# A fused FNet and state-space kernel: the stores of ScalarE move to GpSimd and SyncE

## The chip, the cores and the metric

The kernel runs on one core of one Trainium2 chip. The core has five engines, each with its own instruction stream that it works through in order: TensorE (PE) multiplies matrices, VectorE (DVE) and ScalarE (ACT) do elementwise work, GpSimd (POOL) and SyncE (SP) here mostly issue DMA transfers. Every engine but VectorE and TensorE issues transfers in this kernel. An issue is an instruction of the issuing engine's stream: it waits for what the transfer needs, and what stands behind it on that engine waits too. The transfer itself runs on the core's 16 DMA engines.

The metric is the device time of one execution in microseconds (us).

## The reference

Two independent parts of the same shape, 2048 positions by 512 channels in 32-bit floats, whose outputs are put side by side.

```python
def _A_ref(x, dft_seq_re, dft_seq_im, dft_hid_re, dft_hid_im):      # FNet
    a = jnp.einsum("bsd,ed->bse", x, dft_hid_re)
    b = jnp.einsum("bsd,ed->bse", x, dft_hid_im)
    return jnp.einsum("ts,bse->bte", dft_seq_re, a) - jnp.einsum("ts,bse->bte", dft_seq_im, b)

def _B_ref(u, log_A_real, A_imag, C_real, C_imag, log_dt, D_skip):  # state space
    dt = jnp.exp(log_dt)
    A = -jnp.exp(log_A_real) + 1j * A_imag
    C = (C_real + 1j * C_imag) * dt[:, None]
    P = jnp.exp((A * dt[:, None])[:, :, None] * pos[None, None, :])
    K = 2.0 * jnp.einsum("dn,dnl->dl", C, P).real
    y = jnp.fft.irfft(jnp.fft.rfft(u_t, 2 * L) * jnp.fft.rfft(K, 2 * L)[None], 2 * L)[:, :, :L]
    return y.transpose(0, 2, 1) + u * D_skip[None, None, :]
```

The first part is a Fourier transform over positions and channels, of which only the real part is kept, written as matrix products. The second builds a convolution kernel K of length 2048 for every channel out of 128 complex exponentials, and convolves each channel of u with it through a Fourier transform of length 4096.

## The kernel before

**FNet part** (class `Fnet`). Every 32-bit matrix is split into a rounded high part and a remainder (`hi` and `lo`; ACT makes `hi` at L192, DVE `lo` at L196), and a product is three matmuls at L309. There are twelve groups: eight of kind "s" (four column blocks t, real and imaginary part c), which multiply the sequence matrix by x over 16 slices, and four of kind "p", which multiply those results by the hidden matrix over 8 slices. A group keeps four accumulators d in PSUM, one per 128 rows. Its slices come through SP (L280, tile `raw`, four buffers, of 256 KB each); the splits have three buffers. When a group ends, `evacuate` copies each accumulator out (ACT, L323) into a tile `y`, of which there are three buffers, and stores it: an "s" group's into an intermediate tensor `p` (L328), read back later as `raw`, a "p" group's into the output (L331). The next group's first matmul into an accumulator waits for its eviction.

**State-space part** (class `Ssm`). Tables of exponentials are built in 16 chunks of 32 channels by doubling, mostly on DVE (L541, L550, L557 to L570, with seeds from ACT at L585 to L617); two chunks at a time go through TensorE into taps (L738), and through the first stage of the transform (L768), whose result ACT copies into `xk_sb` and four transfers store to an intermediate tensor `xk` (L785). In the first 100 us the inputs u pass the same first stage in eight steps (L814): POOL loads them (L808), ACT evicts, two transfers per tile store to `xu` (L831). Then for each quarter h of the channels and each q of four groups of frequencies: POOL loads `xu` and `xk` in transposed order (L878), TensorE does the second stage (L907), ACT evicts (L918), DVE multiplies the spectra (L929 to L945), TensorE runs the first inverse stage (L952), ACT evicts into `z` (L967) and two transfers store to `zs` (L973). The last stage loads `zs` (POOL; L1000 for h below 3, L1008 for h = 3, one fetch per q), multiplies (L1023), evicts and stores to the output (L1041; L1034 for h = 3). Tile `z` has one buffer for h below 3 and two for h = 3, and the same buffers hold a product of the spectra in between.

**The order of the work.** All of this is written as Python generators that yield what they need next: an engine with an estimated duration, a buffer, or an event. The class `Plan` runs them on its own clock and emits the instructions in the order in which the plan starts them. So each engine's stream is fixed beforehand. Transfers are one resource in the plan, "dma", whichever engine issues them: a change of the issuing engine leaves the planned order as it is, and moves the instruction into another engine's stream at the same place of that order.

**Who issues what before.** SP issues the slices (`raw`) and constants, POOL the loads of the state-space part (L532 for parameters, L808, L878, L1000, L1008) and eight small additions (L761), ACT the stores at L328, L331, L785, L831, L973 and L1041, and one transfer at each end (L276, L1034).

Of the kernel before, what the change touches and what calls it, by code (L numbers as in the profile page):

```python
# [153 lines left out]
def act(cols):  # L154
    return 0.09 + cols * 0.00085


def dve(cols, rate=1.0):
    return (62 + cols / rate) / 960


def load(kb):
    return max(0.55, kb / 330)


class Fnet:
# [152 lines left out]
    def evacuate(self, g, d, ps):  # L319
        yield self.ys  # L320
        y = self.pool.tile([128, DM], F32, name="y", bufs=STAGED)
        yield "act", act(512)
        self.nc.scalar.activation(y, ps, AF.Copy, scale=-1.0 if g[2] == 1 else 1.0)  # L323
        self.plan.put(self.acc)
        yield "dma", load(256)
        kind, t, c = g
        if kind == "s":
            self.nc.scalar.dma_start(self.p[t, c, d], y)  # L328
            self.plan.set(self.p_ev[t, c, d])
        else:  # L330
            self.nc.scalar.dma_start(self.out[128 * d:128 * d + 128, 512 * t:512 * t + 512], y)  # L331
        self.plan.put(self.ys)


# [27 lines left out]
class Ssm:  # L362
# [393 lines left out]
    def stage1_k(self, ks, n, ev):  # L756

        nc = self.nc
        yield ev
        yield "pool", 0.2  # L760
        nc.gpsimd.tensor_tensor(ks[:, :, 0], self.dskip[:, 16 * n:16 * n + 16], ks[:, :, 0], op=OP.add)  # L761
        yield self.const_ev
        got = yield from self.banks(2)
        yield "pe", 1.82
        for a in range(2):
            for j in range(4):
                r = slice(32 * j, 32 * j + 32)
                nc.tensor.matmul(got[j // 2][1][:, j % 2], self.f1k[r, a], ks[r, :, 32 * a:32 * a + 32],  # L768
                                 start=a == 0, stop=a == 1, tile_position=(32 * j, 0))
        self.plan.put(self.kss)  # L770
        if n == 7:
            self.plan.set(self.k_ev)
        yield self.xks
        xs = self.tab.tile([128, 32, 64], F32, name="xk_sb")
        for h, (k, p) in enumerate(got):
            for j in range(2):
                yield "act", act(512)
                o = 32 * h + 16 * j
                nc.scalar.activation(xs[:, :, o:o + 16], p[:, j].rearrange("p (i l) -> p l i", i=16), AF.Copy)
            self.give(k)  # L780
        xk = self.xk[n // 2].rearrange("b l c s d -> b (c s) l d")[..., 64 * (n % 2):64 * (n % 2) + 64]
        yield "dma", load(1400)
        for k in range(4):
            l = slice(16 * (k // 2), 16 * (k // 2) + 16)
            nc.scalar.dma_start(xk[k % 2, :, l], xs[64 * (k % 2):64 * (k % 2) + 64, l])  # L785
        self.plan.put(self.xks)
        if n % 2:
            self.plan.set(self.xk_ev[n // 2])
        if n == 7:
            self.plan.set(self.tab_ev)  # L790
# [37 lines left out]
    def store_u(self, x, m, sem):  # L828
        yield "dma", load(512)
        for b in range(2):  # L830
            self.nc.scalar.dma_start(self.xu[b, 2 * m:2 * m + 2].rearrange("l c s d -> (c s) l d"),  # L831
                                     x[64 * b:64 * b + 64])
        self.plan.put(sem)
        self.uleft -= 1
        if not self.uleft:
            self.plan.put(self.zls)
            self.plan.set(self.xu_ev)
# [58 lines left out]
    def product(self, b, h, q, got, done):  # L896
        nc, v, a = self.nc, self.nc.vector, self.nc.scalar
        uk = b.pool.tile([128, 2, 2, 2, 2, PART], F32, name="uk", bufs=b.un)
        yield "pe", 1.86
        for r in range(2):  # L900
            for n, name in enumerate("uk"):
                xt = self.xt[name, h, q]
                for c in range(2):
                    for xx in range(4):
                        for g in range(2):
                            rows, o = slice(64 * g, 64 * g + 64), (2 * n + c) * PART
                            nc.tensor.matmul(got[r][1][32 * xx:32 * xx + 32, g, o:o + PART],  # L907
                                             self.w2[rows, 8 * q + 4 * r + xx, 32 * c:32 * c + 32], xt[rows, r, xx],
                                             start=True, stop=True, tile_position=(64 * g, 32 * xx))
        for name in "uk":  # L910
            self.plan.put(b.xts[name])
        self.plan.set(done)
        u, t = uk[:, :, :, 0], uk[:, :, :, 1]
        evs = [Event(), Event()]

        def evict(r, k, p):
            yield "act", act(1024)
            a.activation(uk[:, r].rearrange("p g n c d -> p g (n c d)"), p, AF.Copy)  # L918
            self.give(k)
            self.plan.set(evs[r])  # L920
        for r in range(2):
            self.plan.spawn(evict(r, *got[r]), 1)
        yield b.zbs
        P = b.pool.tile([128, 2, 2, 2, PART], F32, name="z", bufs=b.zn)
        W = b.pool.tile([128, 2, 2, PART], F32, name="w", bufs=b.n)
        for r in range(2):
            yield evs[r]
            yield "dve", dve(512), *APART
            v.tensor_tensor(P[:, r], t[:, r], u[:, r, 0:1].to_broadcast([128, 2, 2, PART]), op=OP.mult)  # L929
        yield "dve", dve(512), *APART  # L930
        v.tensor_tensor(W, t[:, :, 0], u[:, :, 1], op=OP.mult)
        yield "dve", dve(512)
        v.tensor_tensor(P[:, :, 1], P[:, :, 1], W, op=OP.add)
        yield "dve", dve(512), *APART
        v.tensor_tensor(W, t[:, :, 0], u[:, :, 1, ::-1], op=OP.mult)
        for r in range(2):
            yield "dve", dve(512), *APART
            v.tensor_tensor(t[:, r], t[:, r], u[:, r, 0:1, ::-1].to_broadcast([128, 2, 2, PART]), op=OP.mult)
        yield "dve", dve(512), *APART
        v.tensor_tensor(u[:, :, :, 0], P[:, :, :, 0], P[:, :, :, 1], op=OP.subtract)  # L940
        self.plan.put(b.zbs)
        yield "dve", dve(512), *APART
        v.tensor_tensor(t[:, :, 1], t[:, :, 1], W, op=OP.add)
        yield "dve", dve(512)
        v.tensor_tensor(t[:, :, :, 0], t[:, :, :, 0], t[:, :, :, 1], op=OP.add)  # L945

        def run(got):
            for c, Y in enumerate((u, t)):
                for g in range(2):
                    for xx in range(4):  # L950
                        rows = slice(32 * xx, 32 * xx + 32)
                        nc.tensor.matmul(got[xx // 2][1][64 * g:64 * g + 64, xx % 2, :2 * PART], self.ia[rows, c],  # L952
                                         Y[rows, :, g, 0], start=c == 0, stop=c == 1, tile_position=(32 * xx, 64 * g))
        w = Joined(self, run)
        if self.taps_left > 1:
            self.waiting.append(w)
            yield w
        if w.got is None:
            got = yield from self.banks(2)
            yield "pe", 0.95  # L960
            w.run(got, False)
        self.plan.put(b.uks)
        yield b.zbs
        z = b.pool.tile([128, 2, 4, PART], F32, name="z", bufs=b.zn)
        for n, (k, p) in enumerate(w.got):
            yield "act", act(512)
            a.activation(z[:, :, 2 * n:2 * n + 2].rearrange("p r x d -> p x r d"),  # L967
                         p[:, :, :2 * PART].rearrange("p x (r d) -> p x r d", r=2), AF.Copy)
            w.leave(k)
        view = self.zs[h].rearrange("b s q c l d -> b q (c l) s d")  # L970
        yield "dma", load(512)
        for g in range(2):
            nc.scalar.dma_start(view[g, q], z[64 * g:64 * g + 64].rearrange("p r x d -> p (r x) d"))  # L973
        self.plan.put(b.zbs)
        if h == 3:
            self.plan.set(self.zq_ev[q])
        self.left[h] -= 1
        if not self.left[h]:
            self.plan.set(self.zs_ev[h])
# [34 lines left out]
    def inverse(self, z, h, i):  # L1014

        nc, n, m = self.nc, 16, 4
        (k, ps), = yield from self.banks(1)
        yield "pe", 0.95
        for w in range(m):
            for j in range(4):  # L1020
                for g in range(2):
                    rows, l = slice(64 * g, 64 * g + 64), 4 * w + j
                    nc.tensor.matmul(ps[32 * j:32 * j + 32, g, PART * w:PART * w + PART], self.ib[rows, n * i + l],  # L1023
                                     z[rows, l], start=True, stop=True, tile_position=(64 * g, 32 * j))
        y = self.out[:, :, m * i:m * i + m, PART * h:PART * h + PART]
# [12 lines left out]
            nc.scalar.activation(*part(g), AF.Copy)  # L1038
        self.give(k)
        yield "dma", load(512)  # L1040
        nc.scalar.dma_start(y, z[:, :2 * m].rearrange("p (g w) d -> p g w d", g=2))  # L1041
        self.plan.put(self.zls)


# [76 lines left out]
```

## Time and profile before

| | |
|---|---|
| median of 3 runs | 634.37 us (633.76 to 634.55) |
| profiled execution | 630.61 us, of which the span from the first to the last instruction is 628.8 |
| TensorE busy | 583.5 us, 93% of the span |
| VectorE busy | 537.5 us, 85% |
| ScalarE busy | 378.8 us, 60% |
| GpSimd busy | 50.9 us, 8% |
| moved by DMA | 125.43 MB |
| granted TensorE clock, mean | 0.976 |

In lines of the profile L309 is line 309 of the kernel; `acc<-hi,x_hi` is an instruction that writes tile `acc` and reads `hi` and `x_hi`. PE, PEld, DVE, ACT and POOL are busy times of the engines (PEld is the weight load, which overlaps). A "q" behind an engine's name (ACTq, SPq) marks instructions of its sequencer, such as the issue of a transfer, which aren't counted as busy; the issue on POOL is. "x32" is a count. Behind "|" stand the busy time in us and the mean of one instruction in ns, then the idle time of the engine just before and what ended it. In the view of waits "PE acc L309 <- ACT y L323: 8.6, 7, 4.2" says that PE stood idle before L309 for 8.6 us in 7 cases, the longest of 4.2, until ACT had done L323. In a timeline the columns are start, duration, engine, line, operation, tiles and count, with the idle time before in brackets. In sums by stretches each engine has its busy us and its count of instructions, and behind them stand the granted clock, the DMA share and GB/s.

### The profile page before, as it was taken

How to read it: one execution, taken by the hardware profiler on the slowest of the kernel's cores; microseconds unless marked ns; L12 is line 12 of the kernel's file. 1: busy time of each engine (PE TensorE's matmuls, PEld its weight loads, DVE VectorE, ACT ScalarE, POOL GpSimd, SP SyncE). 2: the span in 40 equal slices, each digit the busy share in tenths (PEclk: the TensorE clock that was granted, in tenths of full speed). 3: DMA queues.
4: the chain of work that ended last, by engine and by line, in shares of the span. 5: the costliest groups of instructions: out<-in, count | busy, mean ns of one | idle time of the engine just before them, and what ended most of it. 6: DMA issues, size and time to landing. Idle time of an engine off the chain costs nothing. (4 is left out here: it accounts for less than half of the span.)

```text
span 628.8 us, 17602 instructions
## 1 busy us (share of the span) xinstructions
PE 583.5 (93%) x7302; PEld 445.7 (71%) x7302; DVE 537.5 (85%) x948; ACT 378.8 (60%) x743; POOL 50.9 (8%) x84
## 2 busy tenths in 40 slices
PE   7999999999899999997999899999999999999862
PEld 4877757777588867885788667867777777776641
DVE  5899959989899999998799899999999999639530
ACT  4589876847756566656474667585765554445330
POOL 0000000000010010010011101000100100030110
PEclk7999999999999999999799999999999999999996
DMA  8899987553473375537576567457788685897685
GB/s 270 280 310 303 314 288 221 171 134 106 106 238 103 93 199 160 176 87 186 174 214 209 144 199 178 131 169 184 227 262 266 186 228 158 227 305 247 176 202 147
DMA packets 107983, 125.43 MB, mean 199 GB/s; under 512 B 40000, under 2 KB 67008, under 8 KB 107648
## 3 DMA queue, kind: packets, MB, share of 16 engines
q1 hardware_dynamic: 31168, 52.74, 27.4%
q10 hardware_dynamic: 68608, 41.43, 24.3%
q0 software_dynamic: 8128, 30.15, 15.6%
q8 instruction: 57, 0.93, 0.6%
q14 instruction: 22, 0.18, 0.1%
HBM read 81.56 MB, written 42.73 MB: 198 GB/s over the span
## 5 line engine op out<-in xcount | busy, mean ns | idle before, releaser
L309 PE MATMUL acc<-hi,x_hi 128*128 128x512 f32 x640 | 261.2, 408 | 14.2 <-ACT y L323 8.6
L309 PE MATMUL acc<-lo,x_hi 128*128 128x512 f32 x640 | 253.1, 395 | 1.8 <-DVE lo L196 1.7
L309 PE MATMUL acc<-hi,x_lo 128*128 128x512 f32 x640 | 252.3, 394 | 0.0
L541 DVE TENSOR_TENSOR prod<-t,cs 128x1024 f32<-128x1024 f32 (+4 forms) x192 | 164.8, 869 | 9.2 <-ACT t L680 5.6
L309 PEld LDWEIGHTS acc<-hi,x_hi 128*128 128x128 f32 x640 | 121.8, 190 | 64.6 <-issue 19.2
L192 ACT ACTIVATE hi<-raw 128x512 fp32r<-128x512 f32 x160 | 99.0, 627 | 96.9 <-PE acc L309 64.2
L196 DVE TENSOR_TENSOR lo<-raw,hi 128x512 fp32r<-128x512 f32 x160 | 108.8, 686 | 40.5 <-ACT hi L192 40.2
L309 PEld LDWEIGHTS acc<-lo,x_hi 128*128 128x128 f32 x640 | 122.0, 191 | 27.7 <-DVE lo L196 4.5
L309 PEld LDWEIGHTS acc<-hi,x_lo 128*128 128x128 f32 x640 | 121.7, 190 | 26.7 <-DVE x_lo L196 0.3
L550 DVE TENSOR_TENSOR t<-prod 128x512 f32<-128x512 f32 (+3 forms) x192 | 94.9, 511 | 1.3
L557 ACT ACTIVATE square<-t 128x256 f32<-128x256 f32 (+1 forms) x64 | 36.6, 571 | 23.1 <-DVE t L550 17.8
L323 ACT ACTIVATE y<-acc 128x512 f32<-128x512 f32 x48 | 28.3, 593 | 16.3 <-PE acc L309 9.3
L918 ACT ACTIVATE uk<-f 128x1024 f32<-128x1024 f32 x32 | 31.6, 1014 | 6.8 <-PE f L907 6.8
L738 PEld LDWEIGHTS f<-t,t 128*32 128x32 f32 x2048 | 29.5, 110 | 8.4 <-issue 5.6
L738 PE MATMUL f<-t,t 128*32 128x64 f32 x2048 | 32.4, 220 | 2.0 <-issue 1.8
L617 ACT ACTIVATE cs<-cs 128x352 f32<-128x352 f32 x32 | 15.4, 535 | 21.6 <-DVE cs L612 21.6
L570 DVE TENSOR_TENSOR t<-square 128x128 f32<-128x128 f32 (+1 forms) x64 | 24.7, 386 | 1.4 <-ACT square L557 1.3
L929 DVE TENSOR_TENSOR z<-uk 128x512 f32<-128x512 f32 x32 | 21.3, 686 | 4.3 <-ACT uk L918 4.0
L967 ACT ACTIVATE z<-f 128x512 f32<-128x512 f32 x32 | 17.5, 588 | 11.7 <-issue 4.6
L878 POOL DMA_DIRECT2D xt_u<-xu x13 | 11.8, 908 | 152.7 <-PE f L907 135.8
L599 ACT ACT_TABLE_LOAD x16 | 20.5, 1283 | 5.4 <-DMA xk<-xk_sb 4.8
L907 PE MATMUL f<-xt_k,w 64*32 64x128 f32 x1088 | 23.1, 271 | 0.5 <-issue 0.5
(100 smaller groups left out, 521.5 us busy)
## 6 DMA issues: line engine op xcount, KB each, us to landing
raw<-in_sT SPq DMA_DIRECT2D x127, 256.0 KB, 3.4
p<-y ACTq DMA_DIRECT2D x32, 256.0 KB, 4.1
xk<-xk_sb ACTq DMA_DIRECT2D x32, 256.0 KB, 5.1
xt_k<-xk POOLq DMA_DIRECT2D x16, 512.0 KB, 6.6
zs<-z ACTq DMA_DIRECT2D x32, 256.0 KB, 4.5
raw<-p SPq DMA_DIRECT2D x32, 256.0 KB, 4.1
xt_u<-xu POOLq DMA_DIRECT2D x13, 512.0 KB, 6.4
zl<-zs POOLq DMA_DIRECT2D x12, 512.0 KB, 6.4
```

Of the source, the lines that this page charges most:

```text
L192: self.nc.scalar.activation(hi, src, AF.Copy)
L196: self.nc.vector.tensor_tensor(lo, src, hi.bitcast(F32), op=OP.subtract)
L309: nc.tensor.matmul(acc[d], l[:, cols], r, start=k == 0 and n == 0, stop=k == len(items) - 1 and n == 2)
L323: self.nc.scalar.activation(y, ps, AF.Copy, scale=-1.0 if g[2] == 1 else 1.0)
L541: self.nc.vector.tensor_tensor(p.rearrange("p k d c m -> p k (d c) m"), src.rearrange("p d c l -> p (d c) l")[:, None, :, rows].to_broadca ...
L550: self.nc.vector.tensor_tensor(dst[:, :, :, rows], p[:, 0], p[:, 1, :, ::-1], op=OP.add)
L557: self.nc.scalar.activation(sq, t[:, :, :, m // 2:m], AF.Square)
L570: self.nc.vector.tensor_tensor(t[:, :, 0, m:2 * m:2], box[0][:, :, 0], box[0][:, :, 1], op=OP.subtract)
L738: nc.tensor.matmul(ps[32 * j:32 * j + 32, i], t1[:, d, c], t2[:, d, c], start=c == 0, stop=c == 1, tile_position=(0, 32 * j))
L907: nc.tensor.matmul(got[r][1][32 * xx:32 * xx + 32, g, o:o + PART], self.w2[rows, 8 * q + 4 * r + xx, 32 * c:32 * c + 32], xt[rows, r, xx], ...
L918: a.activation(uk[:, r].rearrange("p g n c d -> p g (n c d)"), p, AF.Copy)
L929: v.tensor_tensor(P[:, r], t[:, r], u[:, r, 0:1].to_broadcast([128, 2, 2, PART]), op=OP.mult)
```

## The change

Six issues change their engine. The stores of the state-space part (`xk`, `xu`, `zs`, and the output for h below 3) are issued by GpSimd, which issues that part's loads; the stores of `y` are issued by SyncE, which issues the `raw` loads. Sizes, tiles, buffers and the planned order stay. The last store of all (L1034) and the very first load (L276) stay on ScalarE.

```diff
@@ Fnet.evacuate
         if kind == "s":
-            self.nc.scalar.dma_start(self.p[t, c, d], y)
+            self.nc.sync.dma_start(self.p[t, c, d], y)
             self.plan.set(self.p_ev[t, c, d])
         else:
-            self.nc.scalar.dma_start(self.out[128 * d:128 * d + 128, 512 * t:512 * t + 512], y)
+            self.nc.sync.dma_start(self.out[128 * d:128 * d + 128, 512 * t:512 * t + 512], y)
@@ Ssm.stage1_k
-            nc.scalar.dma_start(xk[k % 2, :, l], xs[64 * (k % 2):64 * (k % 2) + 64, l])
+            nc.gpsimd.dma_start(xk[k % 2, :, l], xs[64 * (k % 2):64 * (k % 2) + 64, l])
@@ Ssm.store_u
-            self.nc.scalar.dma_start(self.xu[b, 2 * m:2 * m + 2].rearrange("l c s d -> (c s) l d"),
+            self.nc.gpsimd.dma_start(self.xu[b, 2 * m:2 * m + 2].rearrange("l c s d -> (c s) l d"),
                                      x[64 * b:64 * b + 64])
@@ Ssm.product
-            nc.scalar.dma_start(view[g, q], z[64 * g:64 * g + 64].rearrange("p r x d -> p (r x) d"))
+            nc.gpsimd.dma_start(view[g, q], z[64 * g:64 * g + 64].rearrange("p r x d -> p (r x) d"))
@@ Ssm.inverse
-        nc.scalar.dma_start(y, z[:, :2 * m].rearrange("p (g w) d -> p g w d", g=2))
+        nc.gpsimd.dma_start(y, z[:, :2 * m].rearrange("p (g w) d -> p g w d", g=2))
```

## The prediction

> **What bounds the kernel now.** I read the page first, then the waits of PE and of DVE, then sums by stretches of time, and last the timelines around the longest waits.
>
> ```profile
> span 628.8 us, 17602 instructions
> ...
> 100.00:540.00 440.00, 422.43 (x5591) 328.61 (x5590) 415.19 (x724) 272.64 (x543) 35.50 (x53) 0.99 0.62 176
> ...
> PE f L1023 <- DMA zl<-zs: 13.3, 2, 12.6
> PE acc L309 <- ACT y L323: 8.6, 7, 4.2
> PE f L907 <- ACT z L967: 2.7, 2, 2.2
> PE acc L309 <- ACT hi L192: 2.2, 2, 1.8
> ...
> PE f L814 <- ACT ks L748: 1.1, 1, 1.1
> ...
> DVE prod L541 <- ACT t L680: 5.6, 1, 5.6
> ...
> L196 DVE TENSOR_TENSOR lo<-raw,hi 128x512 fp32r<-128x512 f32 x122 | 82.8, 685 | 17.0 <-ACT hi L192 16.9
> ```
>
> The second line is the stretch from 100 to 540 us: TensorE (PE) is busy 422.4 of 440 us, VectorE (DVE) 415.2, ScalarE (ACT) 272.6. Two engines are nearly full and run in a written order; ACT stands between them and is, by its busy time, far from full. Yet the waits name ACT nearly everywhere: in the middle PE waits for evictions (y L323) and splits (hi L192), and DVE stands 16.9 us behind splits in that stretch. Why an engine with spare time is late shows in its own timeline. A DMA that an engine issues isn't counted as busy, but nothing behind it on that engine starts meanwhile:
>
> ```profile
> 291.22 0.63 ACT L323 ACTIVATE y<-acc 128x512 f32<-128x512 f32 x1
> 291.39 5.24 ACTq L785 DMA_DIRECT2D xk<-xk_sb  x4
> 296.66 1.28 ACT L599 ACT_TABLE_LOAD   x1 [4.82 <-DMA xk<-xk_sb]
> ...
> 298.23 0.58 ACT L323 ACTIVATE y<-acc 128x512 f32<-128x512 f32 x1
> ...
> 298.86 0.80 PE L309 MATMUL acc<-hi,x_hi 128*128 128x512 f32 x1 [4.18 <-ACT y L323]
> 301.08 0.79 PE L309 MATMUL acc<-hi,x_hi 128*128 128x512 f32 x1 [0.57 <-ACT y L323]
> ...
> 236.27 0.50 PE L309 MATMUL acc<-hi,x_hi 128*128 128x512 f32 x1 [1.22 <-ACT y L323]
> 238.31 0.50 PE L309 MATMUL acc<-hi,x_hi 128*128 128x512 f32 x1 [1.08 <-ACT y L323]
> ```
>
> Between two evictions of one group ACT issues the four xk stores for 5.24 us; the next eviction starts at 298.23, and PE, which needs that bank, has stood still for 4.18 us. So the bound is the pair PE and DVE, with ACT's issues as the cause of part of their idle time.
>
> **The change part by part.** What leaves ACT:
>
> ```profile
> L785 ACTq DMA_DIRECT2D xk<-xk_sb x32: 596/928/2274, 124.3 to 549.3; - x32
> L973 ACTq DMA_DIRECT2D zs<-z x32: 582/640/1876, 217.3 to 609.2; - x32
> L831 ACTq DMA_DIRECT2D xu<-zl x22: 582/620/1323, 46.9 to 102.4; - x22
> L328 ACTq DMA_DIRECT2D p<-y x32: 326/331/1513, 55.4 to 476.2; - x32
> ```
>
> By counts and medians (the middle of the three ns): 32 x 0.928 = 29.7, 32 x 0.640 = 20.5, the 32 xu stores (22 from zl, 10 from z, at zl's median) x 0.620 = 19.8, 32 x 0.331 = 10.6; the 16 out_ya and 6 out_yb stores come on top. That is at least 81 us of ACT's order, and most of it costs nothing, because splits run ahead of PE. What counts is where someone waits:
>
> *xk stores (L785).* The four PE gaps above sum to 4.18 + 0.57 + 1.22 + 1.08 = 7.05 us; all stand right behind a block of four issues. One more at 170 us ended by a split is the 1.8 of the row "PE acc L309 <- ACT hi L192". Together 8.8 us. The clock adds to it:
>
> ```profile
> 168.70:172.10 3.40, 1.40 (x6) 0.95 (x6) 1.65 (x3) 2.31 (x6) 0.00 (x0) 1.00 0.88 187
> 172.10:175.50 3.40, 3.40 (x10) 2.65 (x9) 3.40 (x7) 1.82 (x5) 1.32 (x2) 0.50 0.89 237
> ...
> 291.00:298.40 7.40, 3.67 (x17) 2.71 (x15) 5.16 (x9) 2.57 (x5) 0.00 (x0) 1.00 0.86 199
> 298.40:305.20 6.80, 5.77 (x13) 4.08 (x14) 4.54 (x7) 4.30 (x9) 0.56 (x1) 0.50 0.82 262
> ```
>
> The first number behind the stretch's length is PE's busy time; the seventh column is the granted clock. After each of the two stretches in which PE was less than half busy the clock is 0.50, for 3.4 and 6.8 us. Half of the busy time there is lost: (3.40 + 5.77) / 2 = 4.6 us. No gap, no such stretch.
>
> *xu stores (L831).* They hold up PE once for 1.1 us (L814) and DVE once for 5.6 us (L541 behind t L680).
>
> So PE is offered 8.8 + 4.6 + 1.1 = 14.5 us. Will DVE follow? It is idle for 440 - 415.2 = 24.8 us in the long stretch, 16.9 of it behind splits; without those some 8 us of idle time are left, so DVE could follow for about 15 us, but then both engines would be without slack at the same time, and each late handover then costs. Ends: 0 (all comes back as waits of PE for DVE) and 14.5. I take two thirds, 9.7 us, nearer to the upper row because in the three largest gaps PE and DVE stand idle together.
>
> *What the stores cost on GpSimd (POOL).* No store is issued there in this trace. The nearest rows:
>
> ```profile
> L878 POOL DMA_DIRECT2D xt_k<-xk x16: 531/561/578, 174.1 to 556.3; - x16
> L878 POOL DMA_DIRECT2D xt_u<-xu x13: 894/907/937, 108.3 to 533.1; - x13
> ...
> zs<-z ACTq DMA_DIRECT2D x32, 256.0 KB, 4.5
> raw<-p SPq DMA_DIRECT2D x32, 256.0 KB, 4.1
> ...
> zl<-zs POOLq DMA_DIRECT2D x8, 256.0 KB, 5.0
> ...
> sum 629.00, PE 583.49 PEld 445.69 DVE 537.48 ACT 378.79 POOL 50.88; mean PE 145.87 PEld 111.42 DVE 134.37 ACT 94.70 POOL 12.72
> ```
>
> A transfer in long rows takes POOL 0.56 us, one in 1024 rows of 512 bytes 0.91. An xk store has 1024 pieces, zs 512, xu 128: Going by pieces I take 0.91, 0.7 and 0.56; with six yb stores of 1024 pieces 32 x (0.91 + 0.7 + 0.56) + 6 x 0.91 = 75 us more on an engine that is busy 50.9 of 629. Its cover is that emptiness: nobody but POOL's own next transfer waits. In written order a POOL load now also stands behind stores: the uG loads by up to 5 us (by the issue times their matmuls start 5 us or more after they would land), the second par load by about 17 (it would still land some 7 us before it is read). Nothing for these; if that cover were gone, PE or DVE would wait for the lateness itself. A store's landing I put 0.5 us later, 5.0 against 4.5 for 256 KB; ends 0 and 0.9 (5.0 against 4.1).
>
> The Trainium skill, "DMA: Bandwidth & Descriptors", section "Issuing engines are not separate DMA queues", says that another issuing engine saves only the sequencer's time to start a transfer, usually small against the transfer. By that rule the gain would be next to nothing; the rows disagree here, since four issues took 5.24 us against a landing of about 5 us for one.
>
> *y on SyncE (SP).* SP's order now mixes y stores with raw loads:
>
> ```profile
> SPq L280 <- DVE lo L196: 382.5, 117, 13.3
> ...
> 290.40 10.60 SPq L280 DMA_DIRECT2D raw<-in_sT  x3
> ...
> 290.41 0.36 ACTq L328 DMA_DIRECT2D p<-y  x1
> ...
> ACT hi L192 <- PE acc L309: 64.2, 49, 3.1
> ```
>
> SP spends most of its time waiting for a free raw buffer, 3.3 us at a time. A y store written behind such a load inherits its wait. In ten of the twelve groups the load ahead of the first store had been issued 1.3 us or more before it; in two (the rows at 290.4 us, and one like it at 350.4) the two fall together. There are three y buffers for four evictions, so the fourth waits for the first store's landing, and PE for the fourth. I charge 1.5 us in all; ends 0 and, if each of the twelve lost its full 3.3 us less about 1 us of slack, 27. The trace is near the low end. The reverse, raw loads behind y stores, is up to 2.7 us, covered by four raw and three split buffers: by the last row, what splits wait for is mostly PE giving a buffer back, not data.
>
> *The tail.*
>
> ```profile
> 592.28 1.08 ACT L967 ACTIVATE z<-f 128x512 f32<-128x512 f32 x2 [3.55 <-DMA zs<-z]
> ...
> 603.82 2.50 ACTq L973 DMA_DIRECT2D zs<-z  x2
> ...
> 607.44 1.08 ACT L967 ACTIVATE z<-f 128x512 f32<-128x512 f32 x2 [0.48 <-PE acc L309]
> ...
> 608.56 1.28 ACTq L973 DMA_DIRECT2D zs<-z  x2
> ...
> 614.46 0.96 POOL L1008 DMA_DIRECT2D zl<-zs  x2 [3.60 <-DMA zs<-z]
> ```
>
> After 607 us PE waits 12.6 us for the last quarter: z eviction, store, fetch, inverse. The last z eviction starts at 607.44 because ACT issued two zs stores for 2.50 us and a y store before it. Without them it starts about 2.4 us earlier; the store costs 0.7 instead of 0.64 per half and lands 0.5 later: 1.8 us gained. In the planner's order both last zs stores stand ahead of the third fetch, so no fetch blocks them; the second quarter's do stand behind the first fetch, 0.3 us. Near 590 us PE waits 2.2 us for a z eviction whose buffer a zs store held; that store now goes ahead of the 1 MB of zl loads in the same queue instead of beside them. Between 0 and 2.2 I take 1.1.
>
> Sum: -9.7 - 1.8 - 1.1 + 1.5 = -11.1 us. The profiled execution took 630.6 us (span 628.8 and 1.8 around it); the median of the runs shown is 634.4, 3.8 above. I keep that difference: 634.4 - 11.1 = 623.3.
>
> **The rivals.**
> *Absorbed:* DVE, 94% busy in the long stretch, takes the place of ACT, and PE's gaps come back as waits for lo or for table tiles. For it: 415.2 of 440. Against it: DVE's own idle time stands behind the same issues. A fifth of 14.5 would be left: 631.5.
> *Hidden anyway:* the issues never ended a wait and the listed releaser is a bystander: 634.4. Against it: the 5.24 us row and both gaps behind it.
> *SP holds y (slower):* the first y store of a group sits behind a raw load, the fourth eviction follows, PE stops at each of 12 group ends. At the mean wait it costs 27 us, so 634.4 - 12.6 + 27 = 649. It outweighs the gain from (12.6 / 12) + 1 = about 2 us of lateness per group. Against it: 1.3 us or more of lead in ten groups.
> *POOL blocks (slower):* a zs store waits behind a load that itself waits for PE; z has one buffer in the first three quarters of the width, so DVE's next product would stand. One such wait of some 5 us for each of 4 quarters costs 20: 634.4 - 12.6 + 20 = 642. Against it: in the old times every POOL instruction written ahead of a store was issued before it, but for two at the end (0.3 and 1.7 us).
> *POOL starved by DVE:* each of the four quarters' stores in the tail waits for a running DVE operation, 4 x 0.7 us (the 685 ns of L196): 626. The Trainium skill, "SBUF — State Buffer", section "A bandwidth-pool intuition that's wrong (but worth ruling out)", tells of GpSimd's descriptor writing blocked until a two-port DVE operation ends; the rows of L878 lie within 894 to 937 ns beside a DVE that is 85% busy, so no such stall shows in this case.
>
> **How the numbers follow.** Chances: forecast 0.62 (its own range 615 to 629: all offers taken give 14.5 + 2.2 + 2.4 = 19; two fifths of the 14.5 and nothing else give 6), absorbed 0.14, starved 0.04, hidden 0.05, SP 0.08, POOL 0.07. Faster by over 0.2% (1.3 us, about what a measurement of this kernel can tell) 0.80, same 0.05, slower 0.15. The range 614 to 636 leaves out the two slow cases and a little below.
>
> **What would show it.** In the changed profile: no ACTq issue but the first raw load and the last out_yb; "PE acc L309 <- ACT y L323" down from 8.6 to under 2; no clock of 0.50 near 172 and 300 us; POOL busy about 126 us; the last z eviction right behind its matmuls. Wrong if PE waits for y evictions at group ends while SP waits for DVE, if POOL's issues take over 1.5 us each, or if PE's new waits name DVE for as much as ACT's go.

## The result and the profile after

The changed kernel takes 608.33 us (median of 4 runs, 606.60 to 613.12) against 634.46 (4 runs beside it): a ratio of 0.9591, 95% interval 0.9524 to 0.9659. In a second comparison it was 610.43, 0.9643 [0.9568, 0.9717]. The forecast was 623.3, the range 614 to 636: the direction was right, the gain more than twice the forecast. The profiled execution took 606.6 us, against 630.6 for that of before.

The page of the changed kernel, span and busy times:

```profile
span 604.5 us, 17668 instructions
...
PE 573.6 (95%) x7302; PEld 441.6 (73%) x7302; DVE 536.1 (89%) x948; ACT 380.7 (63%) x743; POOL 125.0 (21%) x186
```

Of the 24.3 us of span, 583.5 - 573.6 = 9.9 left PE's busy time, though it does the same 7302 instructions, and 14.4 left its idle time. DVE's busy time fell by 1.4, ACT's rose by 1.9. Where the gain lies is seen by cutting both spans at the same places of PE's stream, which is the same in both kernels. Sums by stretches, of before:

```profile
0.00:100.00 100.00, 93.92 (x580) 67.11 (x581) 81.68 (x164) 74.37 (x151) 5.37 (x13) 0.97 0.89 290
100.00:180.00 80.00, 75.46 (x688) 58.02 (x687) 73.74 (x131) 52.52 (x112) 4.56 (x7) 0.98 0.55 152
180.00:290.00 110.00, 107.70 (x1513) 85.04 (x1512) 106.30 (x189) 70.11 (x140) 8.45 (x12) 1.00 0.51 147
290.00:310.00 20.00, 15.24 (x55) 11.60 (x54) 14.54 (x23) 9.05 (x18) 0.56 (x1) 0.83 0.69 193
310.00:540.00 230.00, 224.02 (x3341) 173.95 (x3340) 220.62 (x384) 140.96 (x277) 21.93 (x33) 1.00 0.69 196
540.00:629.00 89.00, 67.13 (x1135) 49.97 (x1133) 40.60 (x62) 31.77 (x51) 10.01 (x19) 0.93 0.75 215
```

And of the changed kernel, cut where the first count in brackets (PE's instructions) agrees with the row above to within two:

```profile
0.00:95.60 95.60, 91.03 (x580) 65.93 (x581) 81.94 (x164) 74.41 (x151) 23.46 (x43) 0.98 0.93 303
95.60:169.50 73.90, 72.15 (x686) 56.91 (x686) 73.50 (x134) 53.36 (x113) 12.30 (x17) 1.00 0.54 160
169.50:279.00 109.50, 107.40 (x1513) 84.56 (x1512) 105.48 (x186) 69.60 (x139) 15.95 (x23) 1.00 0.53 151
279.00:292.20 13.20, 12.24 (x55) 9.78 (x54) 13.10 (x22) 8.56 (x16) 3.28 (x4) 1.00 0.86 215
292.20:518.00 225.80, 222.97 (x3341) 174.29 (x3340) 220.60 (x383) 142.90 (x277) 47.37 (x66) 1.00 0.70 204
518.00:604.50 86.50, 67.83 (x1135) 50.17 (x1133) 41.43 (x64) 31.84 (x51) 22.70 (x35) 0.91 0.75 223
```

The second number of a row is its length. The six stages gain 4.4, 6.1, 0.5, 6.8, 4.2 and, as the span of before ends at 628.8, 2.3 us. In the second and the fourth the granted clock (the third number from the end) rises from 0.98 and 0.83 to 1.00, and DVE is busy for 73.50 of 73.9 and 13.10 of 13.2 us: it has no idle time left there, and the stage is shorter all the same. Each row is one execution. A second profile of the changed kernel, cut in the same way, has 97.0, 74.1, 109.0, 13.3, 226.6 and 88.5 us: stages two and four are the same there, while the first and the last differ by 1.4 and 2.0 us. So the 2.3 us of the last stage are hardly more than two executions differ by.

The view of waits, first of before (a row that the prediction didn't show), then of the changed kernel:

```profile
DVE lo L196 <- ACT hi L192: 40.2, 27, 6.0
```

```profile
PE f L1023 <- DMA zl<-zs: 12.4, 2, 11.7
PE acc L309 <- ACT y L323: 2.6, 2, 1.6
PE f L907 <- DMA xt_k<-xk: 2.5, 2, 2.1
PE acc L309 <- ACT hi L192: 0.2, 1, 0.2
...
DVE lo L196 <- ACT hi L192: 19.9, 15, 3.3
DVE prod L541 <- ACT t L680: 2.6, 1, 2.6
```

PE's wait for evictions fell from 8.6 us to 2.6, that for splits from 2.2 to 0.2. DVE's wait for splits over the whole span halved. New is a wait of 2.5 us for the transposed load of xk.

The place of the largest gap of before (291 to 301 us there), in the changed kernel's timeline:

```profile
280.16 0.63 ACT L323 ACTIVATE y<-acc 128x512 f32<-128x512 f32 x1
280.60 3.28 POOL L785 DMA_DIRECT2D xk<-xk_sb  x4 [8.71 <-ACT xk_sb L779]
280.80 1.28 ACT L599 ACT_TABLE_LOAD   x1
...
282.37 0.58 ACT L323 ACTIVATE y<-acc 128x512 f32<-128x512 f32 x1
...
284.60 0.57 ACT L323 ACTIVATE y<-acc 128x512 f32<-128x512 f32 x1
...
285.23 0.50 PE L309 MATMUL acc<-hi,x_hi 128*128 128x512 f32 x1 [0.96 <-ACT y L323]
```

The four xk stores still take 3.28 us, but on POOL. ACT goes from the eviction to the table load at once and evicts again at 282.37, 2.2 us after the one before instead of 7.0. PE doesn't wait for that eviction any more: the gap of 4.18 us is gone. The gap of 0.96 us stands before the next accumulator, behind the eviction at 284.60, where before had 0.57.

### The profile page after: what moved, and what is told of

The parts are those of the page before. It is cut to its first block, busy times and chain, and to the rows that moved or that the text cites. A ratio compares the mean times of both kernels' runs of the same rounds, so it can differ in the third digit from the quotient of the medians.

```text
span 604.5 us, 17668 instructions
## 1 busy us (share of the span) xinstructions
PE 573.6 (95%) x7302; PEld 441.6 (73%) x7302; DVE 536.1 (89%) x948; ACT 380.7 (63%) x743; POOL 125.0 (21%) x186
## 4 chain that ended last, share of the span: by engine, by line
DVE 37%; PE 34%; DMA 11%; issue 9%; ACT 7%; POOL 1%; SPq 0%; POOLq 0%; ACTq 0%; DVEq 0%
PE acc L309 26%; DVE prod L541 12%; DVE lo L196 7%; DVE t L550 7%; PE f L907 3%; DMA xk<-xk_sb 2%; DMA zl<-zs 2%; DMA zs<-z 2%; DMA xt_k<-xk 2%; PE f L1023 2%; PE f L738 2%; PE f L952 2%; DMA raw<-in_sT 2%; DVE t L570 1%; DVE cs L612 1%
## 5 line engine op out<-in xcount | busy, mean ns | idle before, releaser
L309 PE MATMUL acc<-hi,x_hi 128*128 128x512 f32 x640 | 258.4, 404 | 5.6 <-ACT x_hi L192 2.8
L309 PEld LDWEIGHTS acc<-hi,x_hi 128*128 128x128 f32 x640 | 120.5, 188 | 53.1 <-issue 19.2
L196 DVE TENSOR_TENSOR lo<-raw,hi 128x512 fp32r<-128x512 f32 x160 | 108.8, 685 | 20.1 <-ACT hi L192 19.9
L785 POOL DMA_DIRECT2D xk<-xk_sb x32 | 26.4, 831 | 72.6 <-ACT xk_sb L779 72.6
L918 ACT ACTIVATE uk<-f 128x1024 f32<-128x1024 f32 x32 | 31.7, 1016 | 11.8 <-PE f L907 11.7
L323 ACT ACTIVATE y<-acc 128x512 f32<-128x512 f32 x48 | 28.6, 595 | 14.5 <-PE acc L309 8.4
L973 POOL DMA_DIRECT2D zs<-z x32 | 22.4, 705 | 67.6 <-ACT z L967 61.1
L617 ACT ACTIVATE cs<-cs 128x352 f32<-128x352 f32 x32 | 15.5, 539 | 17.5 <-DVE cs L612 17.4
L1023 PE MATMUL f<-zl,ib 64*32 64x128 f32 x512 | 11.2, 310 | 12.5 <-DMA zl<-zs 12.4
```

The lines of the kernel that those rows point to most:

```text
L196: self.nc.vector.tensor_tensor(lo, src, hi.bitcast(F32), op=OP.subtract)
L309: nc.tensor.matmul(acc[d], l[:, cols], r, start=k == 0 and n == 0, stop=k == len(items) - 1 and n == 2)
L785: nc.gpsimd.dma_start(xk[k % 2, :, l], xs[64 * (k % 2):64 * (k % 2) + 64, l])
```

## The experiments

Theory A: what was lost was lost by ACT's order. A blocked ACT delays evictions, splits and seeds, PE and DVE both stand, and the clock halves after the longest stops. Theory B, the rival: not the place in the order but the transfers themselves matter, which POOL's queue and SP's make in another way (the queues' rows at the end differ greatly). Beside that stood the question of what each part is worth.

**xk alone from GpSimd.** 32 of the moved stores.

```diff
-            nc.scalar.dma_start(xk[k % 2, :, l], xs[64 * (k % 2):64 * (k % 2) + 64, l])
+            nc.gpsimd.dma_start(xk[k % 2, :, l], xs[64 * (k % 2):64 * (k % 2) + 64, l])
```

> The kernel before with the four xk stores alone (L785) issued by GpSimd. Theory A (what counts is ScalarE's order: the time that an issue blocks ScalarE, where TensorE or VectorE waits for the next instruction there): 12 to 16 us faster than before, the waits of TensorE for y evictions under 2 us, no half clock near 172 and 300 us. Theory B (what counts is the transfers: three queues in place of two, other places in the rings, shorter landings): at most 4 us faster, since only 8 of 42 MB of stores move.

Measured: 619.89 us, ratio 0.9798 [0.9726, 0.9871], which is 12.8 us of 634. In its profile no half clock falls near 172 and 300 us, but PE still waits 5.9 us for y evictions, not under 2: the other issues are still ACT's. Cut like the stages above, its gain lies where the stops were. The second stage takes 75.4 us instead of 80, and the fourth:

```profile
285.50:298.80 13.30, 12.33 (x55) 9.89 (x54) 13.20 (x22) 8.64 (x16) 3.28 (x4) 1.00 0.82 200
```

Together that is all of the 11.2 us by which its span is shorter. It holds over all the profiles, each cut where PE has done the same count: in the eight profiles of kernels whose xk stores come from GpSimd, with no copies behind them, the second stage takes 73.9 to 75.4 us and the fourth 13.2 to 13.4; in the five whose xk stores come from ScalarE, 77.8 to 79.9 and 19.1 to 20.1.

**y alone from SyncE.**

```diff
-            self.nc.scalar.dma_start(self.p[t, c, d], y)
+            self.nc.sync.dma_start(self.p[t, c, d], y)
...
-            self.nc.scalar.dma_start(self.out[128 * d:128 * d + 128, 512 * t:512 * t + 512], y)
+            self.nc.sync.dma_start(self.out[128 * d:128 * d + 128, 512 * t:512 * t + 512], y)
```

> The kernel before with the y stores alone (L328, L331) issued by SyncE. Theory A: 2 to 5 us faster (48 issues of 0.33 to 1.5 us leave ScalarE; the waits behind the xk issues stay). Theory B: no change or slower by 1 to 5 us, since y now shares SyncE's ring with the raw loads and lands later.

Measured: 639.92 us (10 runs), ratio 1.0091 [1.0045, 1.0136]: slower by some 5.8 us. This part of the change does harm by itself, against the expectation of theory A and as that of theory B had it. Its timeline at the third block of xk issues:

```profile
296.28 10.68 SPq L328 DMA_DIRECT2D p<-y  x4
...
296.59 5.63 ACTq L785 DMA_DIRECT2D xk<-xk_sb  x4
...
303.82 0.58 ACT L323 ACTIVATE y<-acc 128x512 f32<-128x512 f32 x1
...
304.45 0.79 PE L309 MATMUL acc<-hi,x_hi 128*128 128x512 f32 x1 [4.57 <-ACT y L323]
```

The gap before the eviction stays, since the xk issues stay on ACT, and SP now waits for the same eviction: its four y stores stretch over 10.68 us, with the raw loads behind them.

**xu, zs and the output of h below 3 from GpSimd, xk and y on ScalarE**; then its two halves.

```diff
-            self.nc.scalar.dma_start(self.xu[b, 2 * m:2 * m + 2].rearrange("l c s d -> (c s) l d"),
+            self.nc.gpsimd.dma_start(self.xu[b, 2 * m:2 * m + 2].rearrange("l c s d -> (c s) l d"),
...
-            nc.scalar.dma_start(view[g, q], z[64 * g:64 * g + 64].rearrange("p r x d -> p (r x) d"))
+            nc.gpsimd.dma_start(view[g, q], z[64 * g:64 * g + 64].rearrange("p r x d -> p (r x) d"))
...
-        nc.scalar.dma_start(y, z[:, :2 * m].rearrange("p (g w) d -> p g w d", g=2))
+        nc.gpsimd.dma_start(y, z[:, :2 * m].rearrange("p (g w) d -> p g w d", g=2))
```

> The kernel before with the stores of xu, zs and the h < 3 output alone (L831, L973, L1041) issued by GpSimd. Theory A: 6 to 9 us faster, some 5 of them in the first 116 us (xu) and 1 to 2 in the tail (zs); the waits behind the xk issues and both half-clock stretches stay. Theory B: the larger part of the 26 us, since most of the bytes move here.

Measured: 621.84 us, ratio 0.9814 [0.9743, 0.9886], 11.8 us of 634, nearly as much as xk and more than the 6 to 9 expected. With xu alone (the first pair of lines):

> The kernel before with the 32 xu stores alone (L831) on GpSimd. Theory A: 4 to 5 us faster, all of it before 120 us; the rest of what xu, zs and the output gain together (10.5) then belongs to zs. If the first 100 us are bound by the DMA engines (busy share 0.89 there), no more than 1 us.

Measured: 631.03 us, ratio 0.9957 [0.9918, 0.9996], some 2.7 us. With zs and the output stores alone (the other two pairs):

> Of the change only the zs stores and the out_yb stores of the first three quarters go out from GpSimd; xk, xu and y stay on ScalarE. If the parts are additive and each is worth what ScalarE's order loses by it, this gives what the two together gave less what xu alone gave: 632.4 - 621.8 = 10.5 us less some 1.4 to 3, so 7 to 9 us, a ratio near 0.987. If zs cost nothing in the middle, as the prediction had it, and only the tail gains, it is 1 to 3 us, 0.995 to 0.998.

Measured: 627.45 us, ratio 0.9889 [0.9821, 0.9957], 7.0 us. By this middle value the zs stores are worth more than their place in the tail; the lower end of the interval, 2.7 us, is no more than the tail's 1.8 + 1.1, so that isn't shown. xk (12.8) and the rest of POOL's part (11.8) add up to 24.6, about the whole change (25.9 and 22.6 by its two ratios).

**The issues replaced by work.** The changed kernel, with five copies into an unused tile behind each block of four xk stores. They are the only thing added, and xk goes out from POOL as in the changed kernel.

```diff
+    def busy(self, *cols):
+        src = self.f1k.rearrange("p a b -> p (a b)")
+        for n in cols:
+            self.nc.scalar.activation(self.idle[:, :n].rearrange("p (k m) -> p k m", m=256),
+                                      src[:, None, :].to_broadcast([128, n // 256, 256]), AF.Copy)
...
             nc.gpsimd.dma_start(xk[k % 2, :, l], xs[64 * (k % 2):64 * (k % 2) + 64, l])
+        self.busy(1024, 1024, 1024, 1024, 1024)
```

> The changed kernel with five copies of 128x1024 into an unused tile on ScalarE right behind each four xk issues of GpSimd, so ScalarE is held for about 4.6 us at the old places while the transfers stay on GpSimd. Theory A: the time goes back by what the xk stores alone gain, to 620 to 624 us, with TensorE waiting for y again and the half clock near 300 us again. Theory B: within 2 us of the changed kernel.

Measured: 633.04 us (10 runs), ratio 0.9987 [0.9944, 1.0031]: all the gain is gone. Its timeline at the same place:

```profile
291.12 3.28 POOL L792 DMA_DIRECT2D xk<-xk_sb  x4 [7.85 <-ACT xk_sb L786]
291.17 5.45 ACT L417 ACTIVATE idle<-f1k 128x1024 bf16<-128x1024 f32 x5
...
298.19 0.58 ACT L323 ACTIVATE y<-acc 128x512 f32<-128x512 f32 x1
...
298.82 0.79 PE L309 MATMUL acc<-hi,x_hi 128*128 128x512 f32 x1 [4.40 <-ACT y L323]
...
301.04 0.80 PE L309 MATMUL acc<-hi,x_hi 128*128 128x512 f32 x1 [0.58 <-ACT y L323]
```

(L792 and L786 are L785 and L779 of the changed kernel, moved by the added lines.)

With 5.45 us of copies in place of 5.24 us of issues, PE's gaps are 4.40 and 0.58 us, against 4.18 and 0.57 of before: the same stop, with the transfers on POOL. The stage around it is back at the length and the clock of before:

```profile
289.70:310.10 20.40, 15.42 (x55) 11.70 (x54) 15.04 (x24) 14.01 (x23) 3.85 (x5) 0.83 0.68 191
```

That is theory A; theory B had the gain stay. The loss, 22 to 25 us by the two ratios of the change, is larger than xk's own 12.8. By the parts measured, a kernel with ACT blocked at these places and y on SP keeps xu's and zs's 11.8 less y's 5.8, 6 us; the copies took that too. The traces show a difference that goes this way: the copies hold ACT longer than the issues did. An issue can run beside an instruction that ACT has begun (the issues at 291.39 us in the prediction begin while the eviction of 291.22 still runs). Laid over ACT's own instructions in the trace of before, the 32 xk issues take 36.1 us, of which 30.9 hold ACT alone; the 40 copies hold it for 42.3. In the block shown the two are nearly alike; in the second stage, with the first two blocks, the copies make 83.7 us of 73.9, more than the 80 of before. So the size of this loss is no measure of what xk is worth. That the whole excess comes from the longer hold was not tested.

The same for the other stores of POOL, two copies behind each pair of xu and of zs stores:

```diff
                                      x[64 * b:64 * b + 64])
+        self.busy(1024, 256)
...
             nc.gpsimd.dma_start(view[g, q], z[64 * g:64 * g + 64].rearrange("p r x d -> p (r x) d"))
+        self.busy(1024, 256)
```

> The changed kernel with one copy of 128x1024 and one of 128x256 into an unused tile on ScalarE behind every pair of xu and of zs issues of GpSimd (about 1.35 us each, 32 of them), so ScalarE is held as long as those issues held it. Theory A: 8 to 13 us slower than the changed kernel, about 619. Theory B (the transfers' other queue is what gains): within 2 us of the changed kernel.

Measured: 627.92 us, ratio 0.9898 [0.9859, 0.9937]. By the ratios 16 to 19 us of the gain are lost, where the part alone had given 11.8. Here the copies are no like replacement. Of the 22.7 us of xu issues in the trace of before, 16.0 ran beside ACT's own instructions; the copies behind xu are 23.5 us of ACT's own time, and the first stage takes 109.9 us, longer than the 95.6 of the changed kernel, and longer than the 100 of before too. So this run shows that time in ACT's order costs, with the transfers on POOL, but not how much the xu and zs issues had cost there.

**y in the changed kernel.** The changed kernel with y back on ScalarE, and with y on GpSimd as well:

```diff
-            self.nc.sync.dma_start(self.p[t, c, d], y)
+            self.nc.scalar.dma_start(self.p[t, c, d], y)
```

> The changed kernel with the y stores back on ScalarE; xk, xu, zs and the h < 3 output stay on GpSimd. Theory A (time in ScalarE's order): the gains of the two parts add up, 12.5 + 10.5 = 23 us, so about 610; y on SyncE is then worth 0 to 3 us once nothing else blocks ScalarE. Rival C (y on SyncE costs in itself, because raw loads wait behind y stores that wait for evictions): this kernel is 4 to 8 us faster than the changed one, about 602.

Measured: 612.48 us, ratio 0.9647 [0.9590, 0.9704].

```diff
-            self.nc.sync.dma_start(self.p[t, c, d], y)
+            self.nc.gpsimd.dma_start(self.p[t, c, d], y)
```

> The changed kernel with the y stores on GpSimd too, so that SyncE issues raw loads alone. Theory A: within 2 us of the changed kernel, since ScalarE's order is the same. Rival C: 4 to 8 us faster than the changed kernel, since no raw load stands behind a y store any more.

Measured: 610.44 us, ratio 0.9625 [0.9573, 0.9677]. Both intervals overlap that of the change (0.9591 and 0.9643): who issues y hardly matters once the rest is off ACT, and rival C, with its 4 to 8 us, doesn't show. (In both kernels the out_ya stores move with it.) Then xk from GpSimd and y from SyncE, the other issues on ScalarE:

> xk from GpSimd and y from SyncE; xu and zs stay on ScalarE. If y on SyncE hurts only as long as the xk issues hold ScalarE's evictions, which SyncE's order then waits for, this is as fast as xk alone: ratio 0.976 to 0.983, about 619 to 621 us. If the two are additive (-12.5 for xk, +5.9 for y), it is about 626 us, ratio 0.989.

Measured: 618.72 us, ratio 0.9771 [0.9692, 0.9851]. xk alone had 0.9798: y on SP costs nothing that can be measured here. Had its +5.8 been additive it would be 0.989, outside the interval; but by the intervals of its two parts that sum is itself uncertain by 0.009, so the two nearly touch. Its timeline at the place shown for y alone:

```profile
284.05 5.81 SPq L328 DMA_DIRECT2D p<-y  x4
...
284.93 3.29 POOL L785 DMA_DIRECT2D xk<-xk_sb  x4 [9.05 <-ACT xk_sb L779]
```

SP is through with the four stores in 5.81 us instead of 10.68. Together with the comparison just above, where y on SP costs nothing in the changed kernel, this suggests that y on SP hurts only while ACT's evictions are held up; one of the two alone would hardly carry it. By which path it then hurts stays open. Late raw loads would be the obvious one, but with y alone on SP the waits of ACT's splits for raw are 3.0 us in all, against 5.4 before. What differs most is the clock, a mean of 0.967 against 0.976 in the profiled executions, of which that with y alone was the slowest of its ten; why the clock halves more often there was not found.

**The last quarter's zs stores from SyncE**, as an attempt at the tail, beside the changed kernel once more:

```diff
-            nc.gpsimd.dma_start(view[g, q], z[64 * g:64 * g + 64].rearrange("p r x d -> p (r x) d"))
+            (nc.sync if h == 3 else nc.gpsimd).dma_start(view[g, q], z[64 * g:64 * g + 64].rearrange("p r x d -> p (r x) d"))
```

> The changed kernel with the zs stores of the last quarter (h == 3) issued by SyncE in place of GpSimd. If the end waits for those stores' landing and their fetches behind them, it is 0.5 to 1.5 us faster than the changed kernel beside it, since SyncE's issues are shorter. If SyncE's order (out_ya's last pieces stand ahead of them) holds the stores up, it is 1 to 4 us slower.

> The changed kernel itself, on the same chip as the three beside it: about 608 us, ratio 0.955 to 0.966. A ratio outside this would say that the parts measured on other chips can't be set against one another to better than 1%.

Measured: 612.55 us, 0.9649 [0.9580, 0.9719], against 610.43, 0.9643 [0.9568, 0.9717]: no difference beyond the intervals, and neither of the two expectations for the tail is confirmed. No version beat the changed kernel.

## Why the prediction was right and wrong

**The cause was right.** ACT's blocked order held PE and DVE, and the copies show it. By the signs that the prediction named: no stop at half clock is left near 172 and 300 us (the stages' rows), POOL is busy for 125.0 us where 126 was said. The clearest place is the fourth stage: 20 us before, 13.2 with xk off ACT, 20.4 with copies there and the transfers on POOL. PE's wait for evictions is 2.6 us, not under 2.

**The step that failed first is the discount.** Of 14.5 us offered, two thirds were taken, since DVE, nearly full, would have to follow and "each late handover then costs". It followed: in stages two and four it has no idle time left, and they are 6.1 and 6.8 us shorter. The prediction set one sum of DVE's idle time, 24.8 us over the long stretch, against the offer. Cut by stages, 80 - 73.74 = 6.3 and 20 - 14.54 = 5.5 us of it lie in the two stages with the stops: DVE stood idle there for as long as PE lost, 6.0 and 5.4 us of it behind ACT's splits, and both took up the time together. (The 16.9 us behind splits that the prediction set against 24.8 was read from a view that begins at 80 us; in the long stretch itself it is 15.9. That changes little.) xk was offered 8.8 + 4.6 = 13.4 and gave 12.8 [8.2, 17.4] alone, all of it, by the profile, in these two stages. The whole offer without discount, with the two tail terms, is 17.4 us; still short of 24.

**The xu term was mis-sized: 1.1 us against 4.4 in the first stage.** Only 1.5 of it is idle time; PE's busy time falls by 2.9. Some of that is hidden in rows that look harmless. PE's groups, of before and then of the changed kernel:

```profile
L814 PE MATMUL f<-xt_u,f1u 32*64 32x512 f32 x64 | 6.4, 613 | 1.1 <-ACT ks L748 1.1
L814 PE MATMUL f<-xt_k,f1u 32*64 32x512 f32 x64 | 5.2, 612 | 0.0
```

```profile
L814 PE MATMUL f<-xt_u,f1u 32*64 32x512 f32 x64 | 5.4, 613 | 0.0
L814 PE MATMUL f<-xt_k,f1u 32*64 32x512 f32 x64 | 4.5, 613 | 0.0
```

The same matmuls, 613 ns each, fill 9.9 us instead of 11.6. They overlap, so I read this as lateness that shows as less overlap before it shows as idle time; no run tests that. The low clock at the start is no part of the 4.4 us. The kernel with xk alone on GpSimd issues the same instructions as before in its first 100 us, where no xk store is issued yet; its sums by stretches:

```profile
0.00:100.00 100.00, 94.72 (x578) 66.95 (x579) 81.54 (x164) 73.98 (x151) 5.35 (x13) 1.00 0.89 289
```

The clock is 1.00 there and 0.97 in the profile of before, and yet PE is at the same place after 100 us (578 and 580 instructions). Over all the profiles, the first stage takes 93.1 to 97.0 us in the eight with xu off ACT and no copies behind it, and 99.6 to 104.0 in the five with xu on ACT. Moved alone, xu gave 2.7 us [0.3, 5.2] of the whole time: its first stage was 6.9 us shorter in the profile, but later stages were longer.

**The zs stores in the middle were costed at nothing.** Beyond the tail's 1.8 + 1.1 no zs term was in the sum; zs and the output stores alone gave 7.0 us [2.7, 11.4]. In the change the stage from 310 to 540 us, for which no term stood, gained 4.2. PE's idle time there fell from 230 - 224.02 = 5.98 to 2.83 us, and its waits for evictions (1.1 us for y, 0.5 for z) are gone. I had priced only the few waits of PE over 1 us that named ACT. But one profile doesn't carry a gain of this size: with xu alone on GpSimd, which changes no issue of this stage, it took 236.6 us, 6.6 more than before. The difference of the runs with xu and zs and with xu alone, 11.8 - 2.7 = 9.1 us, speaks for a gain beyond the tail's; how much of it lies in the middle stays open.

**The clock term was mis-sized a little.** 4.6 us were worked out from the stretches at 172 and 298 us. The mean clock over the spans rose from 0.976 to 0.985, a difference of 0.009 x 604.5 = 5.4 us of full clock; but this mean also holds the start and the tail, and was 0.988 in the changed kernel's second profile.

**One cost may have come that was taken as nothing.** The stage from 180 to 290 us holds two of the counted gaps (1.22 and 1.08 us) and gained 0.5. POOL's stores of xk land later, and the load behind them is on PE's path. Timelines of before and of the changed kernel:

```profile
166.63 3.06 ACTq L785 DMA_DIRECT2D xk<-xk_sb  x2
...
174.05 0.57 POOL L878 DMA_DIRECT2D xt_k<-xk  x1 [15.78 <-DMA raw<-in_sT]
```

```profile
156.97 3.32 POOL L785 DMA_DIRECT2D xk<-xk_sb  x4 [6.91 <-ACT xk_sb L779]
...
168.32 0.58 POOL L878 DMA_DIRECT2D xt_k<-xk  x1 [8.03 <-DMA xk<-xk_sb]
```

From the end of the last issue to the load 8.0 us pass instead of 4.4, and PE waits 2.1 us for that load. But waits of 0.9 to 2.1 us for such a load also stand in the four profiles of variants whose xk stores ScalarE issues, so the later landing is not shown to be what kept this stage's gain small. The store's landing had been put 0.5 us later, which holds for zs:

```profile
xk<-xk_sb POOLq DMA_DIRECT2D x32, 256.0 KB, 6.1
...
zs<-z POOLq DMA_DIRECT2D x32, 256.0 KB, 5.0
```

For xk it is 6.1 where ACT's took 5.1.

**Prices on POOL held.** The page's groups of the changed kernel, with 0.83 us for an xk store (0.91 was said) and 0.70 for a zs store (0.7):

```profile
L785 POOL DMA_DIRECT2D xk<-xk_sb x32 | 26.4, 831 | 72.6 <-ACT xk_sb L779 72.6
...
L973 POOL DMA_DIRECT2D zs<-z x32 | 22.4, 705 | 67.6 <-ACT z L967 61.1
```

Neither of the rivals "POOL blocks" and "POOL starved" shows: DVE's product waits for a zs store once, for 1.4 us where that rival had 20.

**The charge for y was +1.5, and the rival "SP holds y" stood at +27.** Alone it is +5.8, in the change nothing that can be measured. The prediction added the parts up; this one depends on another.

**The tail** was to gain 1.8 + 1.1 us, and the last stage gained 2.3 in one profile of the changed kernel and 0.3 in the other; its last z eviction now comes right behind its matmuls, but the wait behind it is still 11.7 us:

```profile
581.83 1.09 ACT L967 ACTIVATE z<-f 128x512 f32<-128x512 f32 x2 [1.22 <-PE f L952]
```

**The rule** of the Trainium skill, "DMA: Bandwidth & Descriptors", section "Issuing engines are not separate DMA queues", that another issuing engine saves only the time to initiate a transfer, usually small: the first half holds, since the transfers got no faster (6.1 us to landing against 5.1 for xk). The second holds for one transfer, 0.93 us of issue against those 5.1, and misleads for this kernel: four issues in a row stood in ACT's order, and copies of about their length cost the whole gain.

## What to carry to other kernels

Count an issue of 0.6 to 1.3 us as work of the engine that issues it, and look for what stands behind it in order and what runs beside it (16.0 of xu's 22.7 us of issues ran beside ACT's own work); an engine at 60% busy can be the one that holds up two full ones. If a cause delays both bounding engines at once, its removal is worth nearly all of the gaps: compare both engines' idle time at the very places of the gaps, stage by stage, before discounting. Parts of a change need not add up: y on SP costs 0.9% while ACT is blocked, and nothing that could be measured when it is not.

## What was not expected of the hardware

The transfers' queues, of before and of the kernel with xk alone on GpSimd (packets, MB, share of the time of 16 engines):

```profile
q10 hardware_dynamic: 68608, 41.43, 24.3%
q0 software_dynamic: 8128, 30.15, 15.6%
```

```profile
q0 software_dynamic: 10688, 38.54, 22.6%
q10 hardware_dynamic: 35328, 33.04, 18.4%
```

The 32 xk stores (8.4 MB) leave 33,280 packets fewer in ACT's queue and 2,560 more in POOL's: 1040 packets a store against 80, and yet they land later.

The clock halves without an idle stretch of its window's length. The row from 168.70 to 172.10 us in the prediction has PE busy for 1.40 of 3.40 us, with no single gap over 1.8, and 0.50 follows. (The other fall, at 298.40 us, comes after 3.4 us in which PE did nothing at all.) In the changed kernel, sums by stretches:

```profile
166.10:169.50 3.40, 1.75 (x8) 1.15 (x7) 3.30 (x8) 1.20 (x3) 1.18 (x2) 1.00 0.82 285
169.50:172.90 3.40, 3.06 (x43) 2.09 (x41) 3.31 (x5) 0.85 (x2) 0.17 (x1) 1.00 0.97 239
```

1.75 of 3.40 is followed by full clock. In these cases the border lies near half of 3.4 us; elsewhere it was not sharp: 2.07 to 2.32 us busy of 3.40 were followed by half clock with zs alone and with y alone moved, and 1.47 by full clock in the kernel with copies behind xu and zs. The Trainium skill, "TensorE: Matmul & The Clock Gate", section "Part 1: The HAM clock gate (the "warmup" mystery)", gives the window of some 3.4 us, which fits the lengths of 3.4 and 6.8 us here, but puts the fall to half clock after an idle window; by the row at 168.70 us a window that is less than half busy can be enough. So a gap of under 2 us can cost nearly as much again: half of the 3.4 us behind it.
